# An attention and MoE kernel on one core: the copied key blocks are filled by transfers between SBUF tiles instead of being loaded and turned

## The chip, the cores and the metric

The kernel runs on one core of a Trainium2 chip. The metric is device time in microseconds (us) of that core, for one launch. Three timed runs of the kernel before stand beside one further execution that was profiled; every duration and every wait quoted below is from that profiled execution.

## What is computed

A banded attention with a few global keys feeds a mixture of experts whose gate is normalised by eight Sinkhorn rounds. Cut to what matters:

```python
# q, k, v: (4 batches, 8 heads, 768, 64); n_global = 8, n_local = 96
scores = (q @ k.T) / sqrt(64)
keep   = (key < n_global) | (0 <= query - key < n_local)
scores = scores - slope[head] * distance          # distance n_local for a global key outside the band
a      = softmax(where(keep, scores, -1e9))
x      = (a @ v) as (3072 tokens, 512)

logits = x @ w_gate;  P = exp(logits - max)       # 8 experts
repeat 8 times: P /= rows' sum; P /= columns' sum; P *= 3072 / 8
out    = sum over e of P[:, e] * (max(x @ w1[e], 0) @ w2[e])    # 512 -> 1024 -> 512
```

All of it is float32. TensorE gets its float32 operands as two rounded parts, hi and lo (`kh` and `kl` for the keys, `qh` and `ql` for the queries), and a product is made of three matmuls: hi with lo, lo with hi, hi with hi.

## The kernel before

The sequence of 768 is six blocks of 128 rows. Attention is cut into 32 **work items**: n = (batch, first or second half of the sequence, pair of heads), four pairs for a half, so items 0 to 3 and 8 to 11 and so on are of a first half, 4 to 7, 12 to 15 and so on of a second half. An item has three query blocks, and each of them, for both heads, is a **group**; so there are 96 groups.

A query block needs its own key block (the diagonal of the band) and a **leading block** of 128 keys: 32 rows of the sequence's first keys (the global ones lie there) and the last 96 rows of the key block before its own. In the raw tile and in the turned tiles an item's blocks are numbered so: of a first half, 0 is the leading block of the third query block and 1 to 3 are own blocks, and the three groups use the blocks [1], [1, 2] and [0, 3]; of a second half, 0, 2 and 4 are leading, 1, 3 and 5 own, and the groups use [0, 1], [2, 3], [4, 5]. So 16 items have four key blocks and 16 have six, though each has only three own ones.

- `load_qk(n)` and `load_v(n)` fetch an item's raw tiles from HBM: every DMA of the attention is issued by SyncE (SP in the profile), from one queue, in the order of SyncE's list. The loads of a second half's leading blocks are L184 (96 rows) and L185 (32 rows), of a first half's L202 and L203. Even items use a stretch of a tile named `acc`, odd items a tile `raw`.
- `prepare(t)` turns an item in three parts. Part 0 is three transposes of q, part 1 four of k (blocks 0 to 3), part 2 two more of k (blocks 4 and 5, second half only). The transposes (L86, `tp<-ident,acc` or `tp<-ident,raw`) write a PSUM tile `tp`; ScalarE copies it to hi (L244) and VectorE subtracts to get lo (L245). Part 2 ends with `load_qk(n + 2)`.
- `scores` (L83, `s_ps`) makes the score matmuls of two groups at a time, four groups ahead of the group that is finished; `softmax`, `turn`, `values` (`o_ps`), `invert` (`r_ps`, L398) and `flush` follow. `flush` writes an item's result to x, hi and lo (`xh`, `xl`), and calls `load_v(n + 2)`.
- `unit(u)` runs four items; eight units make the attention. In the slot of group t it prepares part t + 8 (and t + 9 in the same step of two groups). Between the steps, `between` issues the **spills** (L851: finished `xh`, `xl` and sums of them go to HBM, 384 KB each) and runs **filler**, matmuls of the MoE's first experts (`h_ps`, `y_ps`), from the time that unit 0 is done and the weights are there. Their results `y_sb` go to HBM too (L813, 256 KB). The filler's weights are four pairs of loads `w1f`, `w2f` (L537, L538, 512 KB each) that GpSimd (POOL) splits.

TensorE runs its instructions in the order in which the program is written (`keep_in_program_order`). The order on the other engines, SyncE's list among them, is set by a scheduler that simulates the program's timeline when it is built; so a change at one place moves instructions elsewhere. Eight semaphores, `DMAHW0` to `DMAHW7`, tell that a DMA has landed; SyncE's transfers take them in turn, and a transfer waits until the one eight before it has landed.

After the attention come a transition and then only the MoE's matmuls, which the change doesn't touch.

Of the kernel before, what the change touches and what calls it, by code (L numbers as in the profile page):

```python
# [8 lines left out]
F32 = mybir.dt.float32  # L9
# [3 lines left out]
ALU = mybir.AluOpType  # L13
# [4 lines left out]
P = 128  # L18
BIG = 2.0 ** 100
MAX_LOCAL = 97  # L20
MAX_GLOBAL = 32
SINKHORN_ITERS = 8
EPS = 1e-9
UT = 3
# [8 lines left out]
GROUPS = (((0, 0), (1, 0)), ((0, 1), (1, 1)), ((0, 2), (1, 2)))  # L33
# [55 lines left out]
class Banded:  # L89
# [97 lines left out]
    def heads(self, src, n):  # L187

        b, half, g = self.work[n]
        for j in range(2):  # L190
            yield src[b, 2 * g + j].rearrange("(t p) d -> p t d", p=P), slice(j * self.D, (j + 1) * self.D)

    def load_pair(self, dst, src, n):

        nc, D, G = self.nc, self.D, MAX_GLOBAL
        b, half, g = self.work[n]
        for t, cols in self.heads(src, n):
            self.load_keys(dst, t, half, cols)
        if half == 0:
            both = src[b, 2 * g:2 * g + 2].rearrange("j s d -> s j d")  # L200
            block = dst[:, 0].rearrange("p (j d) -> p j d", j=2)
            nc.sync.dma_start(out=block[0:G], in_=both[0:G])  # L202
            nc.sync.dma_start(out=block[G:], in_=both[P + G:2 * P])  # L203

    def load_qk(self, n):
        if n >= len(self.work):
            return
        half = self.work[n][1]
        t = self.raw_tile(n, 0, 3)
        q_r, k_r = t[:, 0:UT], t[:, UT:]  # L210
        for src, cols in self.heads(self.q, n):
            self.nc.sync.dma_start(out=q_r[:, :, cols], in_=src[:, half * UT:(half + 1) * UT])
        self.load_pair(k_r, self.k, n)
        self.qk[n] = q_r, k_r

    def load_v(self, n):
# [5 lines left out]
    def turned(self, name):  # L222
        ps, tag = self.idle or (self.ps, "tp")
        return ps.tile([P, 4, P], F32, name=name, tag=tag)

    def prepare(self, t):


        n, part = divmod(t, 3)
        if n >= len(self.work):  # L230
            return
        nc = self.nc
        if part == 0:
            self.ready[n] = tuple(self.opd.tile([P, w * UT, P], F32R, name=name)
                                  for name, w in (("qh", 1), ("ql", 1), ("kh", 2), ("kl", 2)))
        q_r, k_r = self.qk[n]
        qh, ql, kh, kl = self.ready[n]
        nk = self.key_blocks(self.work[n][1])[0]
        src, hi, lo, n0, n1 = ((q_r, qh, ql, 0, UT), (k_r, kh, kl, 0, 4), (k_r, kh, kl, 4, nk))[part]
        if n1 > n0:  # L240
            tp = self.turned("tp")
            for t in range(n0, n1):
                self.pe.transpose(out=tp[:, t - n0], in_=src[:, t], identity=self.ident)
            nc.scalar.copy(out=hi[:, n0:n1], in_=tp[:, 0:n1 - n0])  # L244
            nc.vector.tensor_tensor(out=lo[:, n0:n1], in0=tp[:, 0:n1 - n0], in1=hi[:, n0:n1], op=ALU.subtract)  # L245
        if part == 2:
            self.load_qk(n + 2)

    def scores(self, ts):

# [249 lines left out]
class Moe:  # L500
# [40 lines left out]
    def split(self, hi, lo, full):  # L541
        self.nc.scalar.copy(out=hi, in_=full)  # L542
        self.nc.gpsimd.tensor_tensor(out=lo, in0=full, in1=hi, op=ALU.subtract)  # L543
# [495 lines left out]
```

## Time and profile before

| | us |
|---|---|
| median of three timed runs | 2252.55 |
| lowest and highest of them | 2250.11, 2252.9 |
| the profiled execution's own time | 2251.75 |
| its span in the profile | 2250.0 |

The span runs from the first to the last instruction that the profile shows; the 1.75 us around it are start and end of the execution. Stretches that the text speaks of, in us from the span's start:

| stretch | what runs there | TensorE busy |
|---|---|---|
| 0 to 62 | unit 0: attention without filler | 46.55 of 62.00 |
| 62 to 340 | attention with filler between its steps | 37.63 of 38.00, then 237.83 of 240.00 |
| 340 to 380 | last filler, sums, gate | 36.95 of 40.00 |
| 380 to 2250 | MoE matmuls | 1863.34 of 1870.00 |

In the profile PE is TensorE, PEld its loading of weights, DVE VectorE, ACT ScalarE, POOL GpSimd, SP SyncE and SPq its DMA queue. L12 is line 12 of the kernel. In a row of a timeline the first number is when it began, the second how long it took in us, then engine, line, operation, the tile written, the tiles read, and in square brackets how long the engine stood idle before and what released it. In a row with `a/b/c` these are the lowest, median and highest ns of one instruction, and then when the first and the last of them began. In a row of waits, `A <- B: x, n, m`, A waited for B x us in all, n times, m us at the longest. In a row of DMA issues the last number is the median us from the issue to the landing.

### The profile page before, as it was taken

What the parts mean: (1) busy time and instruction counts of PE and PEld (TensorE: products, weight loads), DVE (VectorE), ACT (ScalarE), POOL (GpSimd) and SP (SyncE); (2) the same over time, 40 slices, a digit from 0 to 9 for tenths busy, and PEclk for the clock granted to TensorE, in tenths of its full rate; (3) what the DMA queues carried; (4) which work ended last, traced back from release to release, by engine and by line L of the source; (5) the groups of instructions that cost most, each with busy time, mean ns of one, the idle gap of its engine ahead of it and who ended that gap; (6) DMA issues with size and microseconds to landing.
All of it is one profiled execution on the core that took longest, in us unless ns stands there. A gap on an engine that the chain in (4) does not pass through costs nothing.

```text
span 2250.0 us, 31467 instructions
## 1 busy us (share of the span) xinstructions
PE 2222.3 (99%) x12147; PEld 1980.7 (88%) x12147; DVE 1502.6 (67%) x2682; ACT 712.6 (32%) x1592; POOL 819.8 (36%) x655
## 2 busy tenths in 40 slices
PE   7999999999999999999999999999999999999998
PEld 5888888988989989899898989989999899998997
DVE  6555548876766667666666666666676666766665
ACT  6677663232222222222222233222222222222221
POOL 4257346433333333333333233333333333333320
PEclk9999999999999999999999999999999999999999
DMA  6566431101110011100111541110011110111001
GB/s 161 137 174 173 119 98 61 38 29 38 38 38 29 29 38 38 38 29 29 38 38 38 191 175 38 38 38 29 29 38 38 38 29 29 38 38 38 29 20 58
DMA packets 177615, 133.76 MB, mean 59 GB/s; under 512 B 117040, under 2 KB 148784, under 8 KB 177456
## 3 DMA queue, kind: packets, MB, share of 16 engines
q1 hardware_dynamic: 177456, 131.65, 19.5%
q8 instruction: 98, 1.61, 0.3%
q14 instruction: 61, 0.50, 0.1%
HBM read 108.81 MB, written 22.81 MB: 58 GB/s over the span
## 4 chain that ended last, share of the span: by engine, by line
PE 92%; ACT 2%; issue 2%; POOL 2%; DVE 1%; DMA 1%; SPq 0%; ACTq 0%; DVEq 0%; POOLq 0%
PE y_ps L691 15%; PE y_ps L692 15%; PE y_ps L690 15%; PE bank_d L623 4%; PE bank_d L622 4%; PE bank_c L622 4%; PE bank_c L624 4%; PE bank_a L623 4%; PE bank_c L623 4%; PE bank_d L624 4%; PE bank_a L622 4%; PE bank_a L624 4%; PE h_ps L83 2%; PE bank_b L622 2%; PE bank_b L624 2%
## 5 line engine op out<-in xcount | busy, mean ns | idle before, releaser
L942 DVE SCALAR_TENSOR_TENSOR acc<-y_ps,pm,acc 128x512 f32<-128x512 f32 x672 | 500.5, 748 | 327.1 <-PE y_ps L692 324.9
L692 PE MATMUL y_ps<-w2h,hh 128*128 128x512 f32 x1440 | 567.5, 394 | 0.0
L691 PE MATMUL y_ps<-w2h,hl 128*128 128x512 f32 x1440 | 566.9, 394 | 0.0
L690 PE MATMUL y_ps<-w2l,hh 128*128 128x512 f32 x1440 | 561.9, 390 | 0.0
L543 POOL TENSOR_TENSOR w2l<-w2f,w2h 128x1024 fp32r<-128x1024 f32 x60 | 144.5, 2409 | 701.6 <-ACT w2h L542 701.6
L692 PEld LDWEIGHTS y_ps<-w2h,hh 128*128 128x128 f32 x1440 | 270.1, 188 | 53.7
L690 PEld LDWEIGHTS y_ps<-w2l,hh 128*128 128x128 f32 x1440 | 270.4, 188 | 43.7 <-DVE acc L942 0.4
L691 PEld LDWEIGHTS y_ps<-w2h,hl 128*128 128x128 f32 x1440 | 270.0, 188 | 43.4
L565 POOL TENSOR_TENSOR wsum<-w1f 128x256 f32<-128x256 f32 x300 | 224.4, 782 | 220.7 <-DMA w1f<-in_moe_w_dram 220.7
L543 POOL TENSOR_TENSOR wl<-wsum,wh 128x1280 fp32r<-128x1280 f32 x60 | 177.4, 2956 | 281.5 <-ACT wh L542 281.5
L630 ACT ACTIVATE hh<-h 128x384 fp32r<-128x384 f32 x120 | 63.2, 526 | 502.4 <-DVE h L670 501.0
L631 DVE SCALAR_TENSOR_TENSOR hl<-t,hh 128x384 fp32r<-128x384 f32 x120 | 165.3, 1377 | 10.1 <-ACT hh L630 10.0
L622 PE MATMUL bank_c<-xl,wh 128*128 128x384 f32 x480 | 162.0, 337 | 1.6 <-ACT t L663 1.6
L622 PE MATMUL bank_d<-xl,wh 128*128 128x384 f32 x480 | 160.9, 335 | 1.7 <-DVE t L676 1.7
L624 PE MATMUL bank_c<-xh,wh 128*128 128x384 f32 x480 | 161.9, 337 | 0.0
L623 PE MATMUL bank_c<-xh,wl 128*128 128x384 f32 x480 | 161.2, 336 | 0.0
L623 PE MATMUL bank_d<-xh,wl 128*128 128x384 f32 x480 | 161.2, 336 | 0.0
L623 PE MATMUL bank_a<-sh,wl 128*128 128x384 f32 x480 | 161.1, 336 | 0.0
L622 PE MATMUL bank_a<-sl,wh 128*128 128x384 f32 x480 | 161.0, 336 | 0.0
L624 PE MATMUL bank_a<-sh,wh 128*128 128x384 f32 x480 | 160.8, 335 | 0.0
L624 PE MATMUL bank_d<-xh,wh 128*128 128x384 f32 x480 | 160.3, 334 | 0.0
L631 DVE SCALAR_TENSOR_TENSOR hl<-h,hh 128x384 fp32r<-128x384 f32 x120 | 110.4, 920 | 68.7 <-ACT hh L630 68.7
(195 smaller groups left out, 3895.7 us busy)
## 6 DMA issues: line engine op xcount, KB each, us to landing
w1f<-in_moe_w_dram SPq DMA_DIRECT2D x62, 512.0 KB, 3.4
w2f<-in_moe_w_dram SPq DMA_DIRECT2D x62, 512.0 KB, 3.7
out_dram<-acc SPq DMA_DIRECT2D x24, 256.0 KB, 2.9
ys<-y_sb SPq DMA_DIRECT2D x21, 256.0 KB, 2.1
acc<-ys SPq DMA_DIRECT2D x7, 768.0 KB, 4.6
acc<-in_q_dram SPq DMA_DIRECT2D x32, 96.0 KB, 2.7
acc<-in_k_dram SPq DMA_DIRECT2D x32, 96.0 KB, 2.4
acc<-in_v_dram SPq DMA_DIRECT2D x32, 96.0 KB, 2.2
```

Of the source, the lines that this page charges most:

```text
L83: return self.tc.keep_in_program_order(self.engine.matmul(*args, **kw))
L543: self.nc.gpsimd.tensor_tensor(out=lo, in0=full, in1=hi, op=ALU.subtract)
L565: nc.gpsimd.tensor_tensor(out=s[:, n], in0=x, in1=y, op=op)
L622: self.pe.matmul(out, lhsT=hi(c), rhs=xlo(c), start=(first and c == 0), stop=False, skip_group_check=True)
L623: self.pe.matmul(out, lhsT=lo(c), rhs=xhi(c), start=False, stop=False, skip_group_check=True)
L624: self.pe.matmul(out, lhsT=hi(c), rhs=xhi(c), start=False, stop=(last and c == n - 1), skip_group_check=True)
L630: nc.scalar.activation(out=hh, in_=src, func=AF.Relu)
L631: self.latest = nc.vector.scalar_tensor_tensor(out=hl, in0=src, scalar=0.0, in1=hh, op0=ALU.max, op1=ALU.subtract)
L690: self.pe.matmul(y_ps, lhsT=hh[:, cols], rhs=lf, start=(f == 0), stop=False)
L691: self.pe.matmul(y_ps, lhsT=hl[:, cols], rhs=wf, start=False, stop=False)
L692: self.pe.matmul(y_ps, lhsT=hh[:, cols], rhs=wf, start=False, stop=(f == n - 1))
L942: nc.vector.scalar_tensor_tensor(out=a, in0=y_ps, scalar=moe.pm[:, tt, e:e + 1], in1=a, op0=ALU.mult, op1=ALU.add)
```

## The change

The raw tile no longer holds the leading blocks that repeat rows of own blocks. For a first half `load_qk` loads the three own key blocks; for a second half it loads them and one leading block (that of the first of its query blocks), by the new function `load_leading`. `prepare` turns these in part 1: three transposes for a first half, four for a second half, where there were four and six. In a second half one `tp` tile then holds the leading block and the three own ones, and the new `split` copies it in two pieces, blocks 0 and 1, then blocks 3 and 5.

The leading blocks that are left (block 0 of a first half, blocks 2 and 4 of a second half) are filled by DMAs on SyncE's queue from one place of `kh` or `kl` to another: their 32 global columns from the block that holds them, the other 96 from the own block ahead. That is four DMAs an item, two for `kh` and two for `kl`. Behind them, still in part 1, comes `load_qk(n + 2)`; part 2 is empty. `load_v` loads the same as before.

In numbers for the 32 items: 48 transposes go (256 to 208); the DMAs of `load_qk` go from 6 to 4 for a first half (16 to 96 KB each) and from 8 to 6 for a second half; 128 copies between SBUF tiles come. Lines of the kernel after stand as L-numbers in the rows that follow: copies of the 32 columns are L271 (first half) and L274 (second half), of the 96 columns L272 and L275; L218 and L220 are the loads of q and k, L199, L200 those of a leading block, L566 and L567 are `w1f` and `w2f`, L880 a spill, L842 the `y_sb` store.

```diff
@@ -190,27 +190,36 @@
         for j in range(2):
             yield src[b, 2 * g + j].rearrange("(t p) d -> p t d", p=P), slice(j * self.D, (j + 1) * self.D)
 
+    def load_leading(self, dst, src, n, t):
+
+        nc, G = self.nc, MAX_GLOBAL
+        b, _, g = self.work[n]
+        both = src[b, 2 * g:2 * g + 2].rearrange("j s d -> s j d")
+        block = dst.rearrange("p (j d) -> p j d", j=2)
+        nc.sync.dma_start(out=block[0:G], in_=both[0:G])
+        nc.sync.dma_start(out=block[G:], in_=both[t * P + G:(t + 1) * P])
+
     def load_pair(self, dst, src, n):
 
-        nc, D, G = self.nc, self.D, MAX_GLOBAL
-        b, half, g = self.work[n]
+        half = self.work[n][1]
         for t, cols in self.heads(src, n):
             self.load_keys(dst, t, half, cols)
         if half == 0:
-            both = src[b, 2 * g:2 * g + 2].rearrange("j s d -> s j d")
-            block = dst[:, 0].rearrange("p (j d) -> p j d", j=2)
-            nc.sync.dma_start(out=block[0:G], in_=both[0:G])
-            nc.sync.dma_start(out=block[G:], in_=both[P + G:2 * P])
+            self.load_leading(dst[:, 0], src, n, 1)
 
     def load_qk(self, n):
         if n >= len(self.work):
             return
         half = self.work[n][1]
         t = self.raw_tile(n, 0, 3)
-        q_r, k_r = t[:, 0:UT], t[:, UT:]
+        q_r, k_r = t[:, 0:UT], t[:, UT:2 * UT + 1]
+        tiles = slice(half * UT, (half + 1) * UT)
         for src, cols in self.heads(self.q, n):
-            self.nc.sync.dma_start(out=q_r[:, :, cols], in_=src[:, half * UT:(half + 1) * UT])
-        self.load_pair(k_r, self.k, n)
+            self.nc.sync.dma_start(out=q_r[:, :, cols], in_=src[:, tiles])
+        for src, cols in self.heads(self.k, n):
+            self.nc.sync.dma_start(out=k_r[:, 1:, cols], in_=src[:, tiles])
+        if half == 1:
+            self.load_leading(k_r[:, 0], self.k, n, UT - 1)
         self.qk[n] = q_r, k_r
 
     def load_v(self, n):
@@ -223,28 +232,48 @@
         ps, tag = self.idle or (self.ps, "tp")
         return ps.tile([P, 4, P], F32, name=name, tag=tag)
 
+    def split(self, dst, src):
+
+        hi, lo = dst
+        self.nc.scalar.copy(out=hi, in_=src)
+        self.nc.vector.tensor_tensor(out=lo, in0=src, in1=hi, op=ALU.subtract)
+
     def prepare(self, t):
 
 
-        n, part = divmod(t, 3)
-        if n >= len(self.work):
+
+        n, part = divmod(t, len(GROUPS))
+        if n >= len(self.work) or part == 2:
             return
-        nc = self.nc
+        nc, G = self.nc, MAX_GLOBAL
+        half = self.work[n][1]
         if part == 0:
             self.ready[n] = tuple(self.opd.tile([P, w * UT, P], F32R, name=name)
                                   for name, w in (("qh", 1), ("ql", 1), ("kh", 2), ("kl", 2)))
         q_r, k_r = self.qk[n]
         qh, ql, kh, kl = self.ready[n]
-        nk = self.key_blocks(self.work[n][1])[0]
-        src, hi, lo, n0, n1 = ((q_r, qh, ql, 0, UT), (k_r, kh, kl, 0, 4), (k_r, kh, kl, 4, nk))[part]
-        if n1 > n0:
-            tp = self.turned("tp")
-            for t in range(n0, n1):
-                self.pe.transpose(out=tp[:, t - n0], in_=src[:, t], identity=self.ident)
-            nc.scalar.copy(out=hi[:, n0:n1], in_=tp[:, 0:n1 - n0])
-            nc.vector.tensor_tensor(out=lo[:, n0:n1], in0=tp[:, 0:n1 - n0], in1=hi[:, n0:n1], op=ALU.subtract)
-        if part == 2:
-            self.load_qk(n + 2)
+        src, first = (q_r, 0) if part == 0 else (k_r, 1 - half)
+        tp = self.turned("tp")
+        for t in range(first, src.shape[1]):
+            self.pe.transpose(out=tp[:, t], in_=src[:, t], identity=self.ident)
+        if part == 0:
+            self.split((qh, ql), tp[:, 0:UT])
+            return
+        k = (kh, kl)
+        if half == 0:
+            self.split([a[:, 1:4] for a in k], tp[:, 1:4])
+        else:
+            self.split([a[:, 0:2] for a in k], tp[:, 0:2])
+            self.split([a[:, 3::2] for a in k], tp[:, 2:4])
+        for a in k:
+            a = a.bitcast(F32)
+            if half == 0:
+                nc.sync.dma_start(out=a[:, 0, 0:G], in_=a[:, 1, 0:G])
+                nc.sync.dma_start(out=a[:, 0, G:], in_=a[:, 2, G:])
+            else:
+                nc.sync.dma_start(out=a[:, 2::2, 0:G], in_=a[:, 0:1, 0:G].broadcast_to([P, 2, G]))
+                nc.sync.dma_start(out=a[:, 2::2, G:], in_=a[:, 1:4:2, G:])
+        self.load_qk(n + 2)
 
     def scores(self, ts):
```

The scheduler's list moves with it. Three places of it follow; in brackets stands what an instruction waits for.

**First place: SyncE, start of the program,** where q and k of item 7 (tile `raw_751`) are loaded. Before, two spills and one weight load stand ahead of that, and the item's loads follow one another:

```order
L851 DMA xs_0_0_180<-xh 128x768 [waits DMAHW7_49,Activation_49]
L851 DMA xs_0_1_181<-xl 128x768 [waits DMAHW0_49,DVE_49]
L537 DMA w1f<-in_moe_w_dram 128x4x256 [waits DMAHW1_49,Pool_49]
L212 DMA raw_751<-in_q_dram 128x3x64 [waits DMAHW2_49,PE_49]
L212 DMA raw_751<-in_q_dram 128x3x64 [waits DMAHW3_49]
L183 DMA raw_751<-in_k_dram 128x3x64 [waits DMAHW4_49]
```

After, the second weight pair and two spills stand right ahead of the four copies of item 5, which wait for that item's split (ScalarE's for `kh`, VectorE's for `kl`), and the rest of item 7's loads stands behind them:

```order
L566 DMA w1f<-in_moe_w_dram 128x4x256 [waits DMAHW3_49,Pool_49]
L567 DMA w2f<-in_moe_w_dram 128x2x512 [waits DMAHW4_49,Pool_49]
L880 DMA xs_0_0_178<-xh 128x768 [waits DMAHW5_49,Activation_49]
L880 DMA xs_0_1_179<-xl 128x768 [waits DMAHW6_49,DVE_49]
L218 DMA raw_751<-in_q_dram 128x3x64 [waits DMAHW7_49,PE_49]
L274 DMA kh<-kh 128x2x32 [waits DMAHW0_49,Activation_49]
L274 DMA kl<-kl 128x2x32 [waits DMAHW1_49,DVE_49]
L275 DMA kh<-kh 128x2x96 [waits DMAHW2_49,Activation_49]
L275 DMA kl<-kl 128x2x96 [waits DMAHW3_49,DVE_49]
L218 DMA raw_751<-in_q_dram 128x3x64 [waits DMAHW4_49]
```

What moved: the second w1f and its w2f stand two spills and four copies ahead of item 7's second q load; the last copy takes the semaphore (DMAHW3) that this w1f took.

**Second place: TensorE, the scores of item 5's second group** (the first that read blocks 2 and 3), behind transposes of the next item. Before, with the three q transposes ahead of them:

```order
L86 MATMUL tp<-ident,acc 128x128 [waits DMAHW4_49,DMAHW1_49]
L86 MATMUL tp<-ident,acc 128x128 x2
L83 MATMUL s_ps_871<-kl,qh 128x256
L83 MATMUL s_ps_872<-kl,qh 128x256
L83 MATMUL s_ps_871<-kh,ql 128x256
L83 MATMUL s_ps_872<-kh,ql 128x256
```

After:

```order
L86 MATMUL tp<-ident,acc 128x128 [waits DMAHW4_49,DMAHW3_49]
L86 MATMUL tp<-ident,acc 128x128 x2
L83 MATMUL s_ps_879<-kl,qh 128x256 [waits DMAHW3_49,DMAHW1_49]
L83 MATMUL s_ps_880<-kl,qh 128x256
L83 MATMUL s_ps_879<-kh,ql 128x256 [waits DMAHW2_49,DMAHW0_49,Activation_49]
L83 MATMUL s_ps_880<-kh,ql 128x256
```

What moved: the matmuls stand in the same order, and the first that read `kl` and the first that read `kh` now wait for two DMAs each. TensorE's list before and after is the same but for the 48 transposes.

**Third place: SyncE, item 14's loads and copies** (a second half, with filler and spills about). Before, loads of `acc` for a later item stand around a y_sb store and the spill of xl:

```order
L183 DMA acc<-in_v_dram 128x3x64 [waits DMAHW4_49,PE_49]
L184 DMA acc<-in_v_dram 96x3x64 [waits DMAHW5_49]
L185 DMA acc<-in_v_dram 32x3x64 [waits DMAHW6_49]
L813 DMA ys_201<-y_sb 128x512 [waits DMAHW7_49,Activation_49]
L212 DMA acc<-in_q_dram 128x3x64 [waits DMAHW0_49,PE_49]
L851 DMA xs_0_1_181<-xl 128x768 [waits DMAHW1_49,Pool_49]
L212 DMA acc<-in_q_dram 128x3x64 [waits DMAHW2_49]
```

After:

```order
L185 DMA acc<-in_v_dram 32x3x64 [waits DMAHW6_49]
L880 DMA xs_0_1_179<-xl 128x768 [waits DMAHW7_49,Pool_49]
L842 DMA ys_199<-y_sb 128x512 [waits DMAHW0_49,Activation_49]
L274 DMA kh<-kh 128x2x32 [waits DMAHW1_49,Activation_49]
L275 DMA kh<-kh 128x2x96 [waits DMAHW2_49,Activation_49]
L274 DMA kl<-kl 128x2x32 [waits DMAHW3_49,DVE_49]
L275 DMA kl<-kl 128x2x96 [waits DMAHW4_49,DVE_49]
L218 DMA acc<-in_q_dram 128x3x64 [waits DMAHW5_49,PE_49]
```

What moved: the four copies stand behind the spill of xl, which waits for GpSimd, and behind the store, which waits for ScalarE; the q loads stand behind the copies. At item 22 the list reads alike.

## Prediction

> **What bounds the kernel now.** I read the page first: which engine is full, and what the chain that ended last is made of.
>
> ```profile
> PE 2222.3 (99%) x12147; PEld 1980.7 (88%) x12147; DVE 1502.6 (67%) x2682; ACT 712.6 (32%) x1592; POOL 819.8 (36%) x655
> PE 92%; ACT 2%; issue 2%; POOL 2%; DVE 1%; DMA 1%; SPq 0%; ACTq 0%; DVEq 0%; POOLq 0%
> ```
>
> TensorE is busy 99% of the span and makes 92% of the chain. The change touches the attention stage only, so the next view is the busy time in stretches (columns: stretch, its length, then busy us and instructions of PE, PEld, DVE, ACT, POOL, the granted clock, DMA share and GB/s).
>
> ```profile
> 0.00:62.00 62.00, 46.55 (x371) 33.70 (x372) 36.39 (x149) 40.85 (x132) 28.01 (x40) 0.92 0.65 156
> 62.00:100.00 38.00, 37.63 (x324) 32.50 (x324) 20.54 (x71) 25.70 (x78) 1.99 (x2) 1.00 0.52 127
> 100.00:340.00 240.00, 237.83 (x1979) 203.81 (x1976) 128.59 (x449) 166.86 (x506) 135.72 (x75) 1.00 0.52 142
> 340.00:380.00 40.00, 36.95 (x192) 33.30 (x192) 30.58 (x37) 15.26 (x27) 34.27 (x23) 1.00 0.26 86
> ```
>
> There are two regimes. From 62 us on TensorE idles only about 2.5 us in 278, because the filler matmuls of the MoE stand between the attention's steps: there a matmul less is time less. Up to 62 us it idles 15.5 us: there no filler runs, and the time is set by latencies and transfers. A saving in the first regime counts, one in the second counts only if it lies on the wait that ends last.
>
> **The transposes that go.** 16 items of the first half lose one, 16 of the second half lose two: 48. The trace gives 272 ns for one, but they are pipelined, so their price is the spacing, read from the timeline of TensorE:
>
> ```profile
> L86 PE MATMUL tp<-ident,acc x128: 270/272/447, 8.7 to 303.4; 128*128 128x128 f32 x128
> 111.79 0.49 PE L86 MATMUL tp<-ident,acc 128*128 128x128 f32 x3
> 118.42 0.38 PE L86 MATMUL tp<-ident,acc 128*128 128x128 f32 x2
> 112.64 0.60 PE L86 MATMUL tp<-ident,acc 128*128 128x128 f32 x4
> ```
>
> Two take 0.38 us, three 0.49, four 0.60: each adds 0.11 us (0.109 when the matmuls behind are counted too), not 0.27. So 48 x 0.109 = 5.2 us leave TensorE's work, 0.23% of the run, and no more. TensorE's program order changes in nothing else. Ten of them (items 0 to 6) lie before the wait that I find below to set the time near 62 us, so they drop out of the sum: **38 x 0.109 = -4.1 us**.
>
> **The shorter splits.** ACT and DVE copy fewer columns:
>
> ```profile
> L244 ACT CAST kh<-tp x48: 360/586/608, 9.7 to 312.0; 128x512 fp32r<-128x512 f32 x32, 128x256 fp32r<-128x256 f32 x16
> L245 DVE TENSOR_TENSOR kl<-tp,kh x48: 415/691/693, 10.8 to 312.5; 128x512 fp32r<-128x512 f32 x32, 128x256 fp32r<-128x256 f32 x16
> PE s_ps L83 <- DVE kl L245: 6.3, 8, 2.6
> 16.15 0.33 PE L83 MATMUL s_ps<-kl,qh 64*128 64x128 f32 x2 [1.07 <-DVE kl L245]
> 30.14 0.33 PE L83 MATMUL s_ps<-kl,qh 64*128 64x128 f32 x2 [2.56 <-DVE kl L245]
> 45.65 0.39 PE L83 MATMUL s_ps<-kl,qh 64*128 64x256 f32 x2 [1.39 <-DVE kl L245]
> 106.57 0.33 PE L83 MATMUL s_ps<-kl,qh 64*128 64x128 f32 x2 [0.32 <-DVE kl L245]
> ```
>
> TensorE waits 6.3 us for kl in all, 5.0 of it in the three early rows, so 1.3 later, in pieces of up to 0.32. The split of three blocks instead of four ends some 0.24 us sooner (by the ACT step from 360 to 586 ns and the DVE step from 415 to 691 ns for two blocks more, halved), which closes most of the late pieces: **-1.1 us**. ACT and DVE are far from full, so the rest of what they save is worth nothing.
>
> **What the copies cost.** They cost no TensorE time, but the scores of the second group (second half) or third group (first half) now wait for four transfers, which SyncE issues in its own order, one in about 0.5 us (two starts below, 0.52 apart). An SBUF-to-SBUF copy isn't in the trace. The nearest are the small loads (size, and us from issue to landing):
>
> ```profile
> 48.58 0.48 SPq L183 DMA_DIRECT2D raw<-in_k_dram  x1
> 49.10 0.49 SPq L184 DMA_DIRECT2D raw<-in_k_dram  x1
> ...
> acc<-in_k_dram SPq DMA_DIRECT2D x8, 48.0 KB, 1.9
> acc<-in_k_dram SPq DMA_DIRECT2D x16, 24.0 KB, 2.1
> raw<-in_k_dram SPq DMA_DIRECT2D x8, 16.0 KB, 2.2
> g_f<-in_moe_w_gate_dram SPq DMA_DIRECT2D x1, 16.0 KB, 3.2
> ```
>
> From below 1.9 us (the fastest small load), from above 4.4 (twice the 2.2 of such a load); the gate's 32-byte pieces took 3.2. I take 2.2: the copies move 16 to 96 KB in runs of 128 and 384 bytes, next to the loads' 256.
>
> *Undisturbed item.* Item 12, and what the next paragraph needs of item 14 and POOL:
>
> ```profile
> 113.89 0.69 DVE L245 TENSOR_TENSOR kl<-tp,kh 128x512 fp32r<-128x512 f32 x1 [0.51 <-ACT kh L244]
> 120.04 0.28 PE L83 MATMUL s_ps<-kl,qh 64*128 64x256 f32 x2
> 98.01 1.84 POOL L613 TENSOR_TENSOR xsum<-xh 128x768 f32<-128x768 f32 x1 [42.09 <-ACT xh L389]
> 140.14 0.28 PE L83 MATMUL s_ps<-kl,qh 64*128 64x256 f32 x2
> 133.54 1.84 POOL L616 TENSOR_TENSOR xl<-xsum,xh 128x768 fp32r<-128x768 f32 x1
> 136.80 0.48 SPq L851 DMA_DIRECT2D xs<-xl  x1
> ```
>
> Item 12's kl ended at 114.58 us, the scores that now need copies began at 120.04. That leaves 5.4 us; the last copy is issued within 1.5 us and lands by 3.7: hidden. The second DVE piece and TensorE's lead shrink the margin by about 0.5, not to nothing. First-half items need theirs a group later still.
>
> *What stands behind the copies on SyncE.* Copies that wait for kl hold back the q and k loads of item n+2 (whose call moves up a slot, but behind the copies), v loads, spills and weights. Those loads are needed a whole item later, and that is their cover. Per item there are two issues more than before (four copies against two loads less), 64 x 0.5 = 32 us of SyncE over the 340 us: no cost by itself, but less room to catch up. The second weight pair comes later than before; no filler reads it before the second regime. Cost taken: nothing.
>
> *Items 14 and 22.* In the new SP list (order rows above, third place) the spill of xl and a y_sb store stand ahead of item 14's copies, and the spill waits for POOL: 133.54 + 1.84 = 135.38. Six issues of 0.5 us put the last copy at 137.9, landing at 140.1 to 140.4 behind the spill's 384 KB. The scores were at 140.14, and TensorE will be about 1.1 us ahead of POOL by then (8 transposes and 0.24, since POOL's chain began at 98): due at 139.0. So a wait of about 1.1 there, and again at item 22, where the list reads alike: **+2.3 us**, bounds 0 and 4.
>
> *The start, items 5 and 6.* The new list puts w1f and w2f of the second weight pair and two spills right ahead of item 5's copies. What that does to what follows, the trace shows once:
>
> ```profile
> w1f<-in_moe_w_dram SPq DMA_DIRECT2D x1, 512.0 KB, 6.2
> raw<-in_q_dram SPq DMA_DIRECT2D x2, 96.0 KB, 5.6
> raw<-in_q_dram SPq DMA_DIRECT2D x32, 96.0 KB, 2.5
> SPq L185 <- DMA w1f<-in_moe_w_dram: 1.3, 3, 0.6
> 46.00:47.00 1.00, 1.00 (x18) 0.70 (x14) 0.69 (x3) 0.22 (x1) 1.00 (x1) 1.00 0.98 378
> 51.00:52.00 1.00, 1.00 (x18) 0.83 (x13) 0.66 (x2) 0.55 (x2) 0.00 (x0) 1.00 0.99 211
> ```
>
> The 96 KB loads issued right behind w1f landed after 5.6 us instead of the 2.5 of all 32: transfers land in the order of issue, at 211 to 378 GB/s. And SyncE itself stood still until w1f had landed, because the eighth transfer after it takes its semaphore again. In the new list that eighth is item 5's last copy. [...]
>
> ```profile
> 37.38 0.69 DVE L245 TENSOR_TENSOR kl<-tp,kh 128x512 fp32r<-128x512 f32 x1
> 49.67 0.39 PE L83 MATMUL s_ps<-kl,qh 64*128 64x256 f32 x2
> 57.04 0.29 PE L83 MATMUL s_ps<-kl,qh 64*128 64x256 f32 x2
> 59.01 0.51 PE L83 MATMUL o_ps<-acc 128*64 128x128 f32 x5 [1.09 <-DMA acc<-in_v_dram]
> 61.39 0.55 PE L86 MATMUL r_ps<-ident,inv 128*128 128x128 f32 x3 [0.29 <-ACT acc L318]
> ```
>
> Item 4's kl ends at 38.1; its last copy and the ten transfers behind it put w1f at about 44. Then 1.8 MB (w1f, w2f, two spills) at some 280 GB/s, 6.6 us, with 2 us of latency: item 5's copies land near 53, its scores stood at 49.67. SyncE then issues two k loads as the spills land (52.5), two leading-block loads and six v loads (4 us), and item 6's four copies from 57 to 58.7, landing at 60.5; its scores stood at 57.04: 3.5 late. Against that, the wait of 1.09 for v and 0.29 behind it at 59 to 61 us goes, since v is now issued ahead. Net **+2.1 us**, bounds 0 (the early waits for kl shrink and take the rest in) and 4.6 (transfers 2.5 us slower). Item 7 follows behind the third weight pair, with TensorE as late as its copies: no further term.
>
> Sum: -4.1 - 1.1 + 2.3 + 2.1 = -0.8 us on the profiled run's own 2251.75 (span 2250.0 and 1.75 around it), 2250.95. The median shown is 0.8 above that run: **2251.8**. With the bounds of the terms, this case reaches from 2247.5 to 2256.
>
> **Rivals.** *Faster:* the copies never come last. Then all 48 transposes count, the late kl waits go, and so do the 1.4 us at 59 to 61: -5.2 - 1.1 - 1.4 = -7.7, 2244.9. For it: slack of 5.4 us against 3.7, and DMA share only 0.52. Against: the 5.6 us row.
>
> *Slower:* a copy takes 4.4 us rather than 2.2. From a landing time of about 3.5 us on the undisturbed even items of the second half wait too. At 4.4, four of them wait 0.9 each, items 14 and 22 wait 2.2 more each, and the start loses 2.2: 3.6 + 4.4 + 2.2 = +10.2 on the sum, 2262. For it: runs of 128 bytes and the 3.2 us of the gate; against it: the 24 KB loads at 2.1. [...]
>
> *Nothing reaches the end:* the gain of 5.2 vanishes because TensorE wasn't the limit at these places: 2252.5. The third stretch above speaks against it.
>
> **Chances.** Forecast 0.56, faster 0.24, slower 0.17, nothing 0.03. A measurement of this kernel can tell about 0.2% (4.5 us) from no change, so the bounds are 2248.0 and 2257.1. Of the forecast, 0.02 falls below and 0.02 above: faster 0.26, same 0.55, slower 0.19. The range takes in the forecast's own and the faster rival down to 2244.5; the slower rival is left out above 2257.
>
> **What would show it.** Right: tp rows x104 on each side (208), spaced as before; a wait of TensorE's scores for a DMA of kh or kl near 50 and 58 us (3 to 4 us each time or in one) and near 139 and 222 us (about 1 us); none at the other items; 59.01's wait for v gone. Wrong: waits for copies at items 12, 20 and 28 (slower rival), or none at all (faster). A copy's median landing above 3.5 us overturns the sum, and so does a start that has not lost 2 us by item 7's scores (72.17 before).

## The result and the profile after

The kernel after takes 2268.13 us (median of 4, 2266.65 to 2268.95) against 2252.34 (4 runs, 2250.11 to 2252.9): the ratio is 1.0072 with a 95% interval of 1.0058 to 1.0086. It is 15.8 us slower, where 2251.8 was forecast. Its profiled execution took 2266.65 us by its own time, 14.9 more than the one before, with a span of 2264.8.

The page, busy time and chain:

```profile
PE 2225.5 (98%) x12099; PEld 1982.8 (88%) x12099; DVE 1498.9 (66%) x2682; ACT 710.4 (31%) x1592; POOL 818.3 (36%) x655
PE 91%; issue 2%; POOL 2%; ACT 2%; DVE 1%; DMA 1%; SPq 0%; ACTq 0%; POOLq 0%; DVEq 0%
```

48 matmuls are gone (12147 to 12099), and yet TensorE is busy 3.2 us longer: the matmuls that are left ran slower somewhere. The stretches show where (columns as before, the granted clock third from the end):

```profile
0.00:62.00 62.00, 45.14 (x314) 33.10 (x315) 32.89 (x137) 34.83 (x116) 24.44 (x35) 0.79 0.57 143
62.00:100.00 38.00, 35.56 (x307) 30.60 (x307) 18.97 (x69) 25.97 (x79) 3.50 (x5) 0.99 0.57 139
100.00:340.00 240.00, 229.85 (x1902) 196.22 (x1900) 121.92 (x452) 163.80 (x510) 136.37 (x75) 0.99 0.57 152
```

Up to 62 us 57 matmuls fewer begin than before (314 against 371; some ten of them are transposes that are gone), at a clock of 0.79 against 0.92; from 100 to 340 us TensorE stands idle 10 us instead of 2. The view of waits, and the landings of the copies:

```profile
PE s_ps L83 <- DMA kl<-kl: 17.9, 10, 4.3
...
kh<-kh SPq DMA_DIRECT2D x16, 96.0 KB, 2.1
kl<-kl SPq DMA_DIRECT2D x16, 96.0 KB, 2.1
kh<-kh SPq DMA_DIRECT2D x16, 16.0 KB, 2.0
```

A copy lands in about 2 us, as taken; the scores wait for copies ten times, 17.9 us in all. The ones that matter, in TensorE's timeline, each the first matmul of a group that reads copied blocks (items 0, 1, 4, 5, 12, 14, 22 and 30):

```profile
16.86 0.39 PE L83 MATMUL s_ps<-kl,qh 64*128 64x256 f32 x2 [1.47 <-DMA kl<-kl]
22.80 0.58 PE L83 MATMUL s_ps<-kl,qh 64*128 64x256 f32 x2 [1.10 <-DMA kl<-kl]
43.28 0.58 PE L83 MATMUL s_ps<-kl,qh 64*128 64x256 f32 x2 [2.86 <-DMA kl<-kl]
57.45 0.58 PE L83 MATMUL s_ps<-kl,qh 64*128 64x256 f32 x2 [3.71 <-DMA kl<-kl]
127.02 0.38 PE L83 MATMUL s_ps<-kl,qh 64*128 64x256 f32 x2 [0.54 <-DMA kl<-kl]
151.66 0.51 PE L83 MATMUL s_ps<-kl,qh 64*128 64x256 f32 x2 [4.33 <-DMA kl<-kl]
236.80 0.39 PE L83 MATMUL s_ps<-kl,qh 64*128 64x256 f32 x2 [2.51 <-DMA kl<-kl]
320.05 0.38 PE L83 MATMUL s_ps<-kl,qh 64*128 64x256 f32 x2 [0.70 <-DMA kl<-kl]
```

TensorE's program order is the same but for the transposes, so each matmul can be found in both timelines, and the difference of the two starts tells how late the kernel after is at that point:

| matmul | before | after | late by |
|---|---|---|---|
| item 4, second group | 39.42 | 43.28 | 3.9 |
| item 5, second group | 49.67 | 57.45 | 7.8 |
| item 7, second group | 72.17 | 79.17 | 7.0 |
| item 14, second group | 140.14 | 151.66 | 11.5 (7.0 just ahead of it) |
| a t_ps 2 us behind it | 142.00 | 155.12 | 13.1 |
| item 22, second group | 222.61 | 236.80 | 14.2 (11.5 just ahead) |
| a t_ps 2 us behind it | 224.68 | 240.53 | 15.9 |
| last matmul | 2243.22 | 2257.87 | 14.6 |

So the start costs 7.0 us, item 14 costs 4.5 and 1.6 more behind it, item 22 costs 2.7 and 1.7 more behind it, item 30 about 0.8, and between these places 3.7 us are won back. Behind the wait at item 14 the clock is the reason (granted clock, third from the end):

```profile
151.00:152.00 1.00, 0.34 (x4) 0.37 (x6) 0.00 (x0) 0.00 (x0) 0.00 (x0) 0.89 0.52 122
152.00:153.00 1.00, 1.00 (x10) 0.78 (x10) 0.41 (x3) 0.00 (x0) 0.00 (x0) 0.50 0.76 172
...
154.00:155.00 1.00, 1.00 (x9) 0.67 (x6) 0.05 (x2) 1.00 (x6) 0.00 (x0) 0.50 0.82 259
155.00:156.00 1.00, 1.00 (x9) 0.96 (x8) 0.00 (x0) 0.66 (x4) 0.00 (x0) 0.91 0.86 194
```

From 151.8 to 155.2, for some 3.4 us after the idle stretch, TensorE has half its clock. By the table 1.6 us are lost in that time, about half of it. And this is SyncE's queue up to that wait:

```profile
141.70 0.40 SPq L880 DMA_DIRECT2D xs<-xh  x1
142.20 1.30 SPq L183 DMA_DIRECT2D acc<-in_v_dram  x1
...
145.60 0.47 SPq L185 DMA_DIRECT2D acc<-in_v_dram  x1
146.48 0.35 SPq L880 DMA_DIRECT2D xs<-xl  x1
146.93 0.37 SPq L842 DMA_DIRECT2D ys<-y_sb  x1
147.40 0.60 SPq L274 DMA_DIRECT2D kh<-kh  x1
148.09 0.59 SPq L275 DMA_DIRECT2D kh<-kh  x1
148.78 0.59 SPq L274 DMA_DIRECT2D kl<-kl  x1
149.47 0.59 SPq L275 DMA_DIRECT2D kl<-kl  x1
```

The copies are issued from 147.40, although kl had ended at 142.93: SyncE is held by what stands ahead of them. A copy takes 0.69 us from one issue to the next, against the 0.52 of a load.

### The profile page after: what moved, and what is told of

It is laid out like the page before. It is cut to its first block, busy times and chain, and to the rows that moved or that the text cites. A ratio compares the mean times of both kernels' runs of the same rounds, so it can differ in the third digit from the quotient of the medians.

```text
span 2264.8 us, 31610 instructions
## 1 busy us (share of the span) xinstructions
PE 2225.5 (98%) x12099; PEld 1982.8 (88%) x12099; DVE 1498.9 (66%) x2682; ACT 710.4 (31%) x1592; POOL 818.3 (36%) x655
## 4 chain that ended last, share of the span: by engine, by line
PE 91%; issue 2%; POOL 2%; ACT 2%; DVE 1%; DMA 1%; SPq 0%; ACTq 0%; POOLq 0%; DVEq 0%
PE y_ps L720 15%; PE y_ps L721 15%; PE y_ps L719 14%; PE bank_d L652 4%; PE bank_d L651 4%; PE bank_c L651 4%; PE bank_c L653 4%; PE bank_a L652 4%; PE bank_c L652 4%; PE bank_d L653 4%; PE bank_a L651 4%; PE bank_a L653 4%; PE bank_b L651 2%; PE bank_b L653 2%; PE bank_b L652 2%
```

## The experiments

Three questions: what the removed transposes are worth with no copies in the way; whether the start, items 14 and 22 and the clock are separate costs, and what each is made of; and which version keeps the gain. Each kernel is compared with before in its own runs (medians 2252.2 to 2252.5); edits are against the kernel after.

**No copies at all.** The scores of the leading blocks are left out; own blocks stand in for them.

```diff
-        for a in k:
...
-                nc.sync.dma_start(out=a[:, 2::2, G:], in_=a[:, 1:4:2, G:])
-        return 4, [[1], [1, 2], [0, 3]]
+        return 4, [[1], [1, 2], [2, 3]]
-    return 2 * UT, [[2 * n, 2 * n + 1] for n in range(UT)]
+    return 2 * UT, [[0, 1], [1, 3], [3, 5]]
```

> The kernel after without the 128 copies; the key lists name own blocks in place of the leading blocks that nothing fills now ([2,3] in a first half, [1,3] and [3,5] in a second), so the part of the scores that belongs to leading blocks is left out. The matmuls keep their shapes and number. Theory (the 48 transposes were on TensorE's path, and only the waits for the copies ate their gain): 2244 to 2248, 4 to 8 us under before, no wait of s_ps above 1 us after 62 us. Rival (the transposes were not on the path): 2252 plus or minus 1.5.

2242.26 us, ratio 0.9951 (0.9934 to 0.9967): 10.2 us under before, more than expected. The transposes were on the path. What makes the gain larger than 48 of them are worth, the loads that went with them or the start, isn't taken apart here. After 62 us two waits are left on TensorE, none of s_ps:

```profile
PE t_ps L86 <- DVE kl L239: 0.7, 3, 0.2
PE gt_ps L86 <- ACT pT L339: 0.7, 4, 0.2
```

By the starts of equal matmuls the gain is 2.6 us up to 62 us and 4.5 from 100 to 340. But within the latter, 2.0 us are lost between one t_ps and the next, six times 0.33, in the even items of the second halves.

**Items 0 to 7 the old way.** `load_qk_old` and `prepare_old` are the two functions of before.

```diff
+    def old(self, n):
+        return n < 8
...
+        if self.old(n):
+            return self.load_qk_old(n)
...
+        if n < len(self.work) and self.old(n):
+            return self.prepare_old(t)
```

> Items 0 to 7 load and turn their leading blocks as before, items 8 to 31 use copies. Theory (the delay of the start, 7.0 us by item 7's scores, and the waits at items 12, 14, 22 and 30 are separate costs that add): start as before, item 14 and 22 wait as in the kernel after, 2259 to 2262. Rival (what holds SyncE near item 14 comes at its own time, whatever TensorE's start): the start's 7 us come back as longer waits at items 14 and 22, 2265 to 2268.

2259.28 us, 1.0027 (1.0017 to 1.0038): 8.9 under the kernel after, as the theory says. Item 14 waits as in the kernel after, though TensorE reaches it 5.8 us sooner:

```profile
145.77 0.58 PE L83 MATMUL s_ps<-kl,qh 64*128 64x256 f32 x2 [4.21 <-DMA kl<-kl]
```

The start's loss and item 14's are separate and add up. In the profiled execution the start wins 4.9 us: at item 7's scores it is 2.1 us late against before, not 7.0. And item 22 waits 1.69 in place of 2.51, the clock stays at 1.00 behind it, and the 1.7 us there aren't lost.

**Items 0 to 4 the old way.** The same with another limit.

```diff
+        return n < 5
```

> Items 0 to 4 the old way, 5 to 31 as in the kernel after: of the start's copies only those of items 5, 6 and 7 are left. Theory (the start's 7.0 us are two things, waits at items 0, 1 and 4, whose copies follow the split at once and still take longer than the scores leave, and the wait at item 5 behind the weights and spills): item 5 and 6 keep waits of 2 to 4 us in all, 2262 to 2266, between the run with eight old items (2259.3) and the kernel after (2268.1). Rival (item 5's lateness only follows from the earlier ones): no wait there, 2258 to 2260.

2261.21 us, 1.0037 (1.0023 to 1.0051), just under the range of the theory. Item 5 doesn't wait any more, item 6 does:

```profile
60.63 0.39 PE L83 MATMUL s_ps<-kl,qh 64*128 64x256 f32 x2 [2.54 <-DMA kl<-kl]
```

By the medians, copies in items 5 to 7 cost 1.9 us (2261.21 against 2259.28 with eight old items), which is within the spread of single executions (2259.36 to 2261.94 and 2256.43 to 2260.75), and those in items 0 to 4 another 6.9. So most of the loss goes when items 0 to 4 don't copy, and no term of the prediction priced their copies. In the kernel after itself the table above puts 3.9 of the start's 7.8 us on items 0 to 4 and 3.9 on item 5, so a fixed share of each isn't shown. That item 5 no longer waits fits the rival in part, but SyncE's list is another one in this run, with one weight load less ahead of item 5's copies; the two reasons aren't told apart.

**Dummy matmuls in the waits of items 14 and 22.**

```diff
+        warm = {14 * len(GROUPS): 17, 22 * len(GROUPS): 10}.get(ts[0], 0)
         for c in range(0, len(terms), 2):
+            if c and warm:
+                self.keep_warm(self.ps, "tp", warm)
```

> The kernel after with dummy matmuls on TensorE (17 of 512 columns, 4.1 us) ahead of item 14's second-group scores and 10 (2.4 us) ahead of item 22's, where it stood idle for 4.33 and 2.51 us. They compute nothing that is used. Theory (the idle stretch itself makes the granted clock fall to 0.50 for some 3 us afterwards, which costs 1.5 to 2 us more at each place): granted clock stays 1.00 behind both, 2264 to 2266, 3 to 4 us under the kernel after. Rival (the low clock behind the wait has another cause, or the dummies only add): 2268 or more, and 0.50 again.

2265.36 us, 1.0054 (1.0037 to 1.0071), 2.8 under the kernel after. TensorE's timeline at item 14, then the stretch behind it:

```profile
147.64 3.84 PE L83 MATMUL w_ps<-acc 128*128 128x512 bf16 x17
152.23 0.38 PE L83 MATMUL s_ps<-kl,qh 64*128 64x256 f32 x2 [0.75 <-DMA kl<-kl]
```

```profile
153.00:154.00 1.00, 1.00 (x18) 0.83 (x15) 1.00 (x7) 0.67 (x3) 0.00 (x0) 1.00 0.81 189
```

The scores begin 0.57 us later than in the kernel after, and the t_ps of the table (154.19 here) 0.93 us sooner: 1.5 of the 1.6 us behind item 14 are not lost, and by the same count 1.6 of the 1.7 behind item 22. The dummies move no data; what they change is that TensorE wasn't idle, and the clock stays at 1.00. So the low clock is what the 1.6 to 1.7 us behind each of these waits are made of.

**The y_sb stores on ScalarE's queue.**

```diff
-                    nc.sync.dma_start(out=y_spill[u][:, t], in_=y_sb)
+                    nc.scalar.dma_start(out=y_spill[u][:, t], in_=y_sb)
```

> The kernel after with the y_sb stores issued by ScalarE, so that none stands ahead of the copies of items 14 and 22 on SyncE; the spill of xl still does. Theory (SyncE gets to these copies late because its own issues, 0.4 to 0.7 us each, run one after another behind spills that waited): one issue fewer, the waits at items 14 and 22 shrink by about 0.5 us each, to 3.8 and 2.0; 2266 to 2268. Rival (the store ties the copies to the filler that TensorE does just ahead of the scores): the waits fall under 1 us at both, 2258 to 2261.

2265.66 us, 1.0055 (1.0039 to 1.0072): 2.5 under the kernel after, a little below the theory's range. Item 14 still waits 3.67 and item 22 1.90, 0.66 and 0.61 less, about one issue each. The store is not what holds the copies.

**The spills on GpSimd's queue.** The rest of SyncE's list ahead of these copies stays.

```diff
-                nc.sync.dma_start(out=dst.bitcast(F32), in_=src.bitcast(F32))
+                nc.gpsimd.dma_start(out=dst.bitcast(F32), in_=src.bitcast(F32))
```

> The kernel after with all spills (L880) issued by GpSimd, which makes most of what they carry; the rest of SyncE's list keeps its order, y_sb store, six v loads and four k loads ahead of item 14's and 22's copies included. Theory (the spills, which wait for GpSimd and for each other's landing, put SyncE behind there): the waits at items 14 and 22 fall under 1 us and the granted clock stays at 1.00; 2256 to 2260. Rival (the loads and the store ahead of the copies are enough, as they wait for TensorE's buffers): the waits stay above 2 us, 2265 to 2268. In the start item 5's wait of 3.71 should shrink by at most 1 to 2 us by either, as the weight pair stays ahead of its copies.

2260.15 us, 1.0034 (1.0021 to 1.0046), 8.0 under the kernel after. Items 14 and 22:

```profile
149.82 0.39 PE L83 MATMUL s_ps<-kl,qh 64*128 64x256 f32 x2 [1.18 <-DMA kl<-kl]
232.45 0.39 PE L83 MATMUL s_ps<-kl,qh 64*128 64x256 f32 x2 [0.90 <-DMA kl<-kl]
```

From 4.33 and 2.51 to 1.18 and 0.90, and the clock behind them is 1.00. So the spills are the larger part of these waits, though they don't fall quite under 1, as the theory had it; what the rest is made of, the loads and the store ahead or the copies' own issues and landing, this run doesn't take apart. At item 12 the wait grew from 0.54 to 1.96. In the start item 5's wait shrank from 3.71 to 1.56, but item 4's grew from 2.86 to 3.49 and one of 1.64 came at 63.80, so at item 7's scores this run is as late as the kernel after (7.3 us against 7.0).

**ScalarE and VectorE in place of the DMAs.** They write the leading blocks from the same PSUM tile (a first half likewise).

```diff
-                nc.sync.dma_start(out=a[:, 2::2, G:], in_=a[:, 1:4:2, G:])
+            self.split([a[:, 2::2, 0:G] for a in k], tp[:, 0:1, 0:G].broadcast_to([P, 2, G]))
+            self.split([a[:, 2::2, G:] for a in k], tp[:, 1:3, G:])
```

> The kernel after with ScalarE and VectorE filling the leading blocks from the turned blocks in PSUM (four more small instructions on each side per item pair of pieces, 64 on ScalarE and 64 on VectorE in all) in place of the DMAs. Theory (the loss lies in SyncE's queue and the 2 us landings, not in having the blocks made from own ones): 2244 to 2249. Rival (ScalarE and VectorE then end kl some 0.6 to 1 us later and TensorE waits there instead): 2250 to 2255, with waits for kl in the start.

2274.27 us, 1.0094 (1.0077 to 1.0111): slower than the kernel after, against both expectations.

```profile
PE t_ps L86 <- ACT acc L346: 19.4, 16, 1.6
PE t_ps L86 <- DVE kl L239: 4.8, 3, 1.6
```

TensorE now waits for ScalarE's copy of the turned probabilities (L346); that the added instructions stand ahead of this copy on ScalarE had not been counted. ScalarE is free on average (32% of the span before), and not at this place.

**GpSimd in place of the DMAs.** It copies from block to block in SBUF; the other three copies likewise.

```diff
-                nc.sync.dma_start(out=a[:, 2::2, G:], in_=a[:, 1:4:2, G:])
+                nc.gpsimd.tensor_copy(out=a[:, 2::2, G:], in_=a[:, 1:4:2, G:])
```

> The kernel after with GpSimd copying the leading blocks from the own blocks of kh and kl in SBUF in place of the DMAs: 128 small copies on an engine that is idle up to 98 us but for 28 us and busy 57% from 100 to 340 us in pieces of 1.84 us. Theory (what costs is SyncE's list and the landing, and ScalarE, in the way of which the fills of the run with engines stood, is free again): waits only where a fill stands behind GpSimd's long sums, 2246 to 2256. Rival (GpSimd's list holds the fills behind a chain of sums, as SyncE's held the copies behind spills): waits of 2 us and more at items 12 to 15 and 20 to 23, 2258 or more.

2250.0 us, 0.9988 (0.9979 to 0.9998): 2.3 under before, within the theory's range. TensorE's scores wait for GpSimd's fills twice, 1.0 and 0.6 us, both before 62 us; at item 7's scores the run is 2.7 us late against before, and from 100 to 340 it wins 3.2.

**Copies only where nothing waited for them.** The old way for the other items.

```diff
+        return n < 8 or n % 8 in (4, 6)
```

> Copies only in items 8 to 11, 16 to 19, 24 to 27 and the odd items of the second halves from 13 on, where the kernel after showed no wait for them or one of 0.35; items 0 to 7 and the even ones of the second halves load and turn their leading blocks as before. 24 transposes go instead of 48. Theory (the gain of a transpose is 0.11 us wherever no wait takes it back): 24 x 0.11 = 2.6 us and some 0.5 of late kl waits, 2248 to 2251. Rival (the copies' issues alone, SyncE's list and its order, cost time elsewhere): 2253 or more.

2245.89 us, 0.9972 (0.9961 to 0.9983): 6.4 us under before, twice the theory's sum. After 62 us this is all that TensorE waits for by this view:

```profile
PE gt_ps L86 <- ACT pT L388: 0.5, 3, 0.2
```

It wins 5.1 us from 100 to 340, with half the transposes removed: 24 x 0.109 and the 1.3 us of late kl waits make 3.9; where the other 1.2 us come from isn't shown. It keeps the old split in the even items of the second halves, and between t_ps and t_ps no more is lost than before. This is the best kernel of the study that computes everything.

**One split in place of two.** The copied blocks stand at 0 and 1, the turned ones at 2 to 5, and the scores read [2, 3], [0, 4] and [1, 5].

```diff
-            self.split([a[:, 0:2] for a in k], tp[:, 0:2])
-            self.split([a[:, 3::2] for a in k], tp[:, 2:4])
+            self.split([a[:, 2:] for a in k], tp)
```

> The kernel after with the turned blocks of a second half in another order (own blocks and the first leading one at 2 to 5, the copied ones at 0 and 1), so that one split of four blocks takes the place of the two of two; copies as in the kernel after. Theory (the second piece on VectorE ends late and holds the PSUM tile that the next t_ps or tp needs, which showed as 2.0 us more between t_ps and t_ps in 100 to 340 us, in the run without copies too): that gap closes, 2265 to 2267, some 2 us under the kernel after, with the waits for copies as before. Rival (the 2.0 us come from elsewhere): 2268 plus or minus 1 and the same 2.0 us.

2265.62 us, 1.0061 (1.0044 to 1.0078), 2.5 under the kernel after. Between t_ps and t_ps 0.35 us are left of the 2.8 that the kernel after loses there; but the scores of the first group now wait for kl seven times after 62 us, 1.7 us in all, as four blocks take longer than two (691 against 415 ns for VectorE's kl in the kernel before). The two about cancel: at item 22's scores this run is 14.0 us late against before, the kernel after 14.2. Only behind these scores does its profiled execution get ahead, as it waits 1.45 there in place of 2.51 and the clock stays at 1.00. So the gap closed as the theory says, but that this is what made the run faster isn't shown. What VectorE did at item 14 in the kernel after fits the gap:

```profile
142.17 0.42 DVE L321 CUSTOM_DVE_ANT_0 p_sb<-s_ps,acc 128x256 f32<-128x256 f32 x1
142.51 0.08 DVE L321 DVE_READ_ACCUMULATOR2_ANT mx<- 128x1 f32 x1
142.51 0.42 DVE L239 TENSOR_TENSOR kl<-tp,kh 128x256 fp32r<-128x256 f32 x1
```

The second piece stands behind the softmax of three score tiles and ends at 142.93. Eight t_ps begin at 142.43, 0.11 us apart; the fifth needs the PSUM tile that this piece still reads, and begins at 143.08, where 142.92 was due.

**Old way up to item 7, one split and GpSimd's copies from item 8.** The edits of three runs above together.

```diff
+        return n < 8
...
+            self.split([a[:, 2:] for a in k], tp)
...
+                nc.gpsimd.tensor_copy(out=a[:, 0:2, G:], in_=a[:, 3:5, G:])
```

> Items 0 to 7 the old way; from item 8 on the leading blocks are filled by GpSimd from own blocks and a second half's split is one piece. All 36 transposes of the later items go, with no DMA for them. Theory (transposes at 0.11 us are worth their time wherever neither a copy nor the two-piece split is in the way): 3.9 us for the transposes, 1 for late kl waits, 1 to 2 for the start's wait for v: 2244 to 2247. Rival (GpSimd's fills end behind its sums, or what they take from GpSimd delays the sums at the end of the attention): 2249 or more.

2249.82 us, 0.999 (0.998 to 0.9999): not the 2244 to 2247 of the theory. TensorE waits for the longer split nine times:

```profile
PE s_ps L83 <- DVE kl L255: 2.8, 9, 0.5
```

From 100 to 340 us it wins 2.6 us, half of what the run with 24 transposes wins. The rest lies in the start: three kernels in which items 0 to 7 go the old way stand at item 7's scores 3.3 us late (this one), 2.1 late (the one with copies from item 8) and 0.9 early (the one with 18 items), against before. Their granted clock up to 62 us differs (0.83, 0.85 and 0.92 in their profiles); why, no run here settles.

## Why the prediction was wrong, point by point

**What bounds the kernel: right.** TensorE is the limit in the attention stage; without copies, 48 transposes less make 10.2 us, and the forecast's rival without late copies had said 7.7. The other 2.5 have no shown cause.

**The transposes (-4.1) and the shorter splits (-1.1): about right, with a cost missed.** The late kl waits went. The second-half split in two pieces, though, was counted only for what its later end does to the copies. It also holds a PSUM tile that t_ps needs: 2.0 us in the run without copies. One split closes this gap, and costs 1.7 us of waits for kl in its place.

**"I take 2.2" for a landing: right.** Medians of 1.8 to 2.1 us were measured. The slower rival, which ended on the right side, rested on 4.4 and so is wrong as a mechanism. The copies with runs of 128 bytes (16 and 32 KB) landed in 1.8 to 2.0 us, those with runs of 384 bytes (48 and 96 KB) in 1.9 to 2.1.

**"Undisturbed item ... hidden": nearly.** Items 20 and 28 don't wait, item 12 waits 0.54, item 13 0.35.

**Items 14 and 22 (+2.3): the step that failed.** "Six issues of 0.5 us put the last copy at 137.9" was counted from GpSimd's end of the xl that the spill carries, 135.38. GpSimd in the kernel after:

```profile
139.86 1.82 POOL L645 TENSOR_TENSOR xl<-xsum,xh 128x768 fp32r<-128x768 f32 x1
```

It ended at 141.68, 6.3 us later, no more than TensorE itself. But the spill was issued at 146.48, since SyncE got to it only then, 4.8 us behind GpSimd. The prediction's own row of this spill before, issued at 136.80, was 1.4 us behind GpSimd already, and the count didn't use it. What stands ahead on SyncE (four k loads, a spill, six v loads, and before those the spills of the sums) was not walked back. The last row ahead of the spill that waited for an engine was the first v load (142.20), 1.3 us for TensorE; this is SyncE's view of waits from 139 to 152:

```profile
SPq L183 <- PE t_ps L86: 1.3, 1, 1.3
SPq L842 <- ACT qh L238: 0.4, 1, 0.4
```

The waits were 4.33 and 2.51, 6.8 in place of 2.3; moving the spills to another queue took 4.8 of them away. And each cost another 1.6 to 1.7 us by the clock, for which the sum had no term. Together TensorE lost 10.5 us here in place of 2.3: half of the error of 16.3.

**The start (+2.1): mis-sized, for two reasons.** The late copies of item 5 behind the weights came as described (3.71 measured, 3.3 by the prediction's own numbers), but the copies of items 0, 1 and 4 were never set against their scores. The trace of before had it; this is item 4's first matmul of the second group:

```profile
39.42 0.28 PE L83 MATMUL s_ps<-kl,qh 64*128 64x256 f32 x2
```

Its kl ended at 38.1. So 1.3 us were there for copies that take 0.69 from one issue to the next and 2.0 to land: by this matmul the kernel after is 3.9 us late, as much as item 5 adds. Of the 1.4 us that were to come back at 59 to 61, 0.8 had by item 7's scores: the wait for v is gone, but one of 1.25 for ql stands at 65.23. And at a clock that stands at 0.50 from 43 to 49 us and from 57 to 63, at and behind the start's two longest waits (2.86 and 3.71), the lateness is not made up. 7.0 in place of 2.1: another 4.9 us of the error. The two-piece split's 2.0 and item 30's 0.8 make most of the rest.

**SyncE's extra issues "no cost by itself": wrong.** They are part of what makes its list late: at 0.69 us a copy, four copies for two loads add 1.7 us to each item's share of a list in which everything waits its turn. The cover that was named, a whole item of time, holds for loads (after 62 us TensorE waits for none); it doesn't hold for transfers that stand behind them and are needed within an item.

## What to carry to other kernels

A DMA that takes the place of engine work is hidden by its slack against the place in the queue that it gets, not against its own length: walk the issuing queue back to the last issue that really waited, and count every row from there. Here the copies landed in about 2 us, but those of item 14 were first issued 4.5 us after their kl had ended. Price a wait on TensorE with what the clock does behind it, and not only with its length: here 4.33 us of waiting at item 14 cost 1.6 more behind it, and 2.51 at item 22 cost 1.7 more. A trade that pays in some iterations and not in others can be made where the slack is: here the copies in 18 of 32 items gave 6.4 us, and in all 32 they cost 15.8.

## What was not expected of the hardware

An idle stretch of TensorE of 2.51 us (item 22), and of 1.90 us at the same place in the run with the stores moved, was followed by a granted clock of 0.50 for more than 3 us; stretches of 1.69 us (item 22 with eight old items) and of 1.18 and 0.90 us (spills on GpSimd) were not. This is the run with the stores moved, where the 1.90 us of idleness ended at 237.09:

```profile
238.50:239.00 0.50, 0.50 (x8) 0.33 (x3) 0.50 (x3) 0.50 (x3) 0.50 (x1) 0.63 0.95 276
241.00:242.00 1.00, 1.00 (x4) 0.81 (x3) 0.00 (x0) 0.26 (x1) 0.00 (x0) 0.50 0.32 63
242.00:242.50 0.50, 0.50 (x3) 0.38 (x3) 0.00 (x0) 0.00 (x0) 0.00 (x0) 0.96 0.55 128
```

The clock falls between 238.5 and 239, some 1.5 us after the work has begun again, and is back just after 242. So here the fall followed 1.90 us of idleness.

The length of the stretch alone doesn't decide, though. Item 12 in the run with the spills on GpSimd comes first here; then one place behind the attention, where TensorE idles 1.62 us, in the run with copies in 18 items and in the kernel before. Behind each comes the stretch with its granted clock:

```profile
128.73 0.39 PE L83 MATMUL s_ps<-kl,qh 64*128 64x256 f32 x2 [1.96 <-DMA kl<-kl]
128.00:134.00 6.00, 5.27 (x43) 4.75 (x44) 2.09 (x10) 3.31 (x11) 5.88 (x6) 1.00 0.59 192
359.41 0.44 PE L692 MATMUL bank_c<-xl,wh 128*128 128x384 f32 x1 [1.62 <-ACT t L733]
361.00:364.00 3.00, 3.00 (x11) 2.55 (x10) 1.49 (x3) 0.52 (x1) 3.00 (x3) 0.50 0.27 91
365.83 0.44 PE L622 MATMUL bank_c<-xl,wh 128*128 128x384 f32 x1 [1.62 <-ACT t L663]
365.00:370.00 5.00, 4.17 (x23) 3.90 (x24) 3.52 (x6) 1.30 (x3) 5.00 (x4) 1.00 0.11 27
```

So 1.96 us left the clock at 1.00, and 1.62 us at one and the same place were followed by 0.50 in one run and by 1.00 in the other; in the kernel after, the same 1.62 us, up to 380.51, left it at 1.00. How long the low clock lasts differs too: 3.4 us behind item 14 and behind item 22 in the kernel after (151.8 to 155.2 and 237.1 to 240.5), 10.2 us in its start (18.7 to 28.9). What decides this, no run here shows.
